# 640-point transform stages taken three slabs at a time instead of two

## The chip, the core and the metric

The kernel runs on one core of a Trainium2 chip. The metric is device time in microseconds (us), the median of three runs. A profiled execution is one run of its own; its span is the time between its first and last instruction.

## The reference

```
xn = layernorm(x)                                  # x: 2048 x 640, bf16
s  = irfft2(rfft2(xn) * (w_r + 1j*w_i))            # over rows and columns
g  = silu((gelu(xn @ w_gate) * (xn @ w_up)) @ w_down)   # 640 -> 1536 -> 640
out = x + s * g
```

So a spectral filter and a gated feed-forward network (FFN) run on the same normalized input and are multiplied at the end.

## The kernel before

The 2048 rows are held as 16 slabs of 128 rows. Both branches are matmuls. The FFN runs over four groups of four slabs: gate and up products (line 670: `psg`, `psu`), gelu on ScalarE into `ge` (L674), the product `uT` on VectorE (L676), and the down products (L694), whose result goes through tanh or silu into `G` (L702/L703, L699).

The Fourier branch has four stages, which are put in between the FFN's matmuls:

- Forward, per slab: `fold_a` and `fold_b` on VectorE add and subtract mirrored columns of `X` into a tile `f` (L443 to L453); `slab_S1` multiplies `f` with a table (`pz`, L481, five matmuls) and ScalarE copies it out as `Z` (L483). Per two slabs, `pair_D` calls `d_pair`: 128-row matmuls (L490) and then 32-row matmuls (L494) into `pd`, two PSUM tiles of two banks each. The two tiles are copied to `zd` with the columns spread by two (L502), and each slab is stored to DRAM scratch `ZDR` (L504).
- Frequency: `load_B2` reads `ZDR` back in ten DMAs (`B`, L522), in rows that hold all slabs; `pair_S2` multiplies (`px`, L532), copies (`xs`) and filters by `W1`, `W2` (L539); `pair_S2i` multiplies back (`pu`, L552) and stores to `UDR`.
- Inverse: `load_V` reads `UDR`; `slab_S1i` (`pv`, L597; `vs`, L599) per slab; `pair_Di` (again L490/L494) per two slabs, copied out as `eo` (L611); VectorE forms `cs` (L620) and `Yall` (L628/L629); `finish` multiplies by `G`, adds `x` and stores (L645 to L647).

Below, a call of `pair_D` or `pair_Di` is called a *turn*: within it TensorE goes over to 32-row matmuls and back.

The order is written by hand. A list `back` holds the FFN's pieces in order: 144 steps, numbered 0 to 143, each some five 512-column matmuls or eight 320-column ones. `put(s, f, ...)` hangs other work behind step `s`; that work is issued after the step's own matmuls, in the order of the `put` calls. Every engine takes its instructions in that order. The pool `psB` has two PSUM tiles, and `pz`, `pd`, `px`, `pu`, `pv` and the transposes all take turns in them; a turn takes both. Gate and up have two banks each. `load_B2` stands at step 54, the first `pair_S2` at 64, the second at 65, the inverse stage from step 96 (`vs0`). The tables are made in one scratch tile, `GEN`, whose parts are `vt` and `fv`; it, `B2` and `Vin` share one buffer after each other. All DMAs are issued by the SP queue, in order.

The step list of the forward stage, with `F0 = 30`:

```
for pair in range(8):
    a = F0 + 3 * pair
    put(a, slab_S1, 2 * pair)
    put(a + 1, slab_S1, 2 * pair + 1)
    put(a + 2, pair_D, pair)
```

Of the kernel before, what the change touches and what calls it, by code (L numbers as in the profile page):

```python
# [10 lines left out]
BF16 = mybir.dt.bfloat16  # L11
INT32 = mybir.dt.int32
ACT = mybir.ActivationFunctionType
ALU = mybir.AluOpType
P = 128
S = 2048
D = 640
L = 321
LP = 322
LH = 161  # L20
HD = 160
F = 1536
NT = F // P
NS = 16
# [7 lines left out]
def kernel(  # L32
# [40 lines left out]
    with tc.manual_schedule():  # L73
        build(nc, locals())


def build(nc, env):
    consts, big, wts, xg, work, psA, psB = (env[k] for k in ("consts", "big", "wts", "xg", "work", "psA", "psB"))
    ZDR, UDR, X, Wg, Wu, Wd, W1, W2 = (env[k] for k in ("ZDR", "UDR", "X", "Wg", "Wu", "Wd", "W1", "W2"))
# [52 lines left out]
    FT = consts.tile([P, 5, LH], BF16)  # L132
    FI = consts.tile([P, 5, LH], BF16)
# [8 lines left out]
    def gtile(shape, dt):  # L142
        n = 1
        for k in shape:
            n *= k
        w = n if dt != BF16 else n // 2
        ap = GEN[:, goff[0]:goff[0] + w]
        goff[0] += w
        assert goff[0] <= NH * L // 2
        if dt != INT32:  # L150
            ap = ap.bitcast(dt)
        if len(shape) > 1:
            names = "abcdefg"[:len(shape)]
            ap = ap.rearrange("p (%s) -> p %s" % (" ".join(names), " ".join(names)), **dict(zip(names, shape)))
        return ap
# [4 lines left out]
    done = set()  # L160
# [5 lines left out]
    xf = {}  # L166
# [50 lines left out]
    vt = gtile([NS, P], INT32)  # L217
# [111 lines left out]
    fv = gtile([10, LH], FP32)  # L329
# [125 lines left out]
    def chunk(f, k, c):  # L455
        return f[:, k, c * P:(c + 1) * P]
# [16 lines left out]
            nc.scalar.copy(out=xnT[g][:, :, j * P:(j + 1) * P], in_=pt)  # L473

    Zt = {}

    def slab_S1(n1):
        f = xf[n1 // 2]
        pz = psB.tile([P, 5, P], FP32, tag="b")
        for c in range(5):  # L480
            nc.tensor.matmul(pz[:, c, :], lhsT=chunk(f, n1 % 2, c), rhs=Tfwd[:, n1, :], start=True, stop=True)  # L481
        Zt[n1] = work.tile([P, 5, P], BF16, tag="m1", bufs=2, name=f"Z{n1}")
        nc.scalar.copy(out=Zt[n1], in_=pz)  # L483

    def d_pair(lhs, T, w):
        ps = [psB.tile([P, 2, 512], FP32, tag="b", name=f"pd{b}") for b in range(2)]
        out = [[ps[g // 2][:, g % 2, a * w:(a + 1) * w] for g in range(4)] for a in range(2)]
        for a in range(2):
            for g in range(4):
                nc.tensor.matmul(out[a][g], lhsT=lhs[a][:, g, :], rhs=T[:, g, 0:w], start=(a == 0), stop=False)  # L490
        for a in range(2):
            for g in range(4):
                r = slice(32 * g, 32 * g + 32)
                nc.tensor.matmul(out[a][g], lhsT=lhs[a][r, 4, :], rhs=T[r, 4, 0:w], start=False, stop=(a == 1))  # L494
        return [t[:, :, 0:2 * w].rearrange("p k (a m) -> p a k m", a=2) for t in ps]

    def pair_D(pair):
        pd = d_pair([Zt.pop(2 * pair + a) for a in range(2)], FT, LH)
        zd = work.tile([P, 2, 2, LP], BF16, tag="m2", bufs=2)
        for b in range(2):  # L500
            ev = nc.vector.tensor_copy if pair == 1 and b == 1 else nc.scalar.copy
            ev(out=zd.rearrange("p a c (m b) -> p a c m b", b=2)[:, :, :, :, b], in_=pd[b])  # L502
        for a in range(2):
            nc.sync.dma_start(out=ZDR[:, 2 * pair + a].rearrange("c p l -> p c l"), in_=zd[:, a, :, 0:L])  # L504

    warm_bank = []

# [52 lines left out]
    st_c = {}  # L560
# [4 lines left out]
    def load_V():  # L565
# [5 lines left out]
        st_c["V"] = V  # L571
        st_c["Y"] = big.tile([P, NS, D], BF16, tag="sX", name="Yall")

# [18 lines left out]
    def slab_S1i(n1):  # L592
        V = st_c["V"]
        pv = psB.tile([P, 5, P], FP32, tag="b")
        for c in range(5):
            lhsT = V[:, n1, VO[c]:VO[c] + P] if c < 4 else st_c[("r", n1)]
            nc.tensor.matmul(pv[:, c, :], lhsT=lhsT, rhs=Tinv[:, n1, :], start=True, stop=True)  # L597
        vs = work.tile([P, 5, P], BF16, tag="m1", bufs=2)
        nc.scalar.copy(out=vs, in_=pv)  # L599
        st_c[n1] = vs  # L600

    BY_SILU = (0, 3)
    Gt = {}
    Gok = set()

    def pair_Di(pair):
        n0 = 2 * pair
        py = d_pair([st_c.pop(n0 + a) for a in range(2)], FI, HD)
        eo = work.tile([P, 2, 2, 2, HD], BF16, tag="m2", bufs=2)
        for b in range(2):  # L610
            nc.scalar.activation(out=eo[:, b], in_=py[b], func=ACT.Copy,  # L611
                                 scale=(2.0 if n0 // 4 in BY_SILU else 1.0) / (S * D))
        st_c[("e", pair)] = eo

    def pair_cs(pair):
        eo = st_c.pop(("e", pair))
        st_c[("c", pair)] = cs = work.tile([P, 2, 2, 2, HD], BF16, tag="xf", bufs=2, name="cs")
        flat = "p a k n -> p (a k n)"
        for q, op in ((0, ALU.add), (1, ALU.subtract)):
            nc.vector.tensor_tensor(out=cs[:, q].rearrange(flat), in0=eo[:, 0].rearrange(flat),  # L620
                                    in1=eo[:, 1].rearrange(flat), op=op)

    def pair_Y(pair):
        n0 = 2 * pair
        cs = st_c.pop(("c", pair))
        Y = st_c["Y"][:, n0:n0 + 2, :].rearrange("p a (h n) -> p a h n", h=2)
        C, Z = (cs[:, :, :, k, :].rearrange("p h a n -> p a h n") for k in range(2))
        nc.vector.tensor_tensor(out=Y[:, :, :, 0:HD], in0=C, in1=Z, op=ALU.add)  # L628
        nc.vector.tensor_tensor(out=Y[:, :, ::-1, 319:159:-1], in0=C, in1=Z, op=ALU.subtract)  # L629
        for a in range(2):  # L630
            done.add(("y", n0 + a))

    left = {(n1, k) for n1 in range(NS) for k in range(2)}

# [3 lines left out]
    def finish(n1):  # L638
# [4 lines left out]
        G = Gt[n1 // 4]  # L643
        Y = st_c["Y"][:, n1, sl]
        nc.vector.tensor_tensor(out=Y, in0=Y, in1=G[:, n1 % 4, sl], op=ALU.mult)  # L645
        nc.vector.tensor_tensor(out=Y, in0=Y, in1=xts[n1][:, sl], op=ALU.add)  # L646
        nc.sync.dma_start(out=outv[n1][:, sl], in_=Y)  # L647
# [103 lines left out]
    def put(s, *item):  # L751
        plan[s].append(item)
# [35 lines left out]
    put(27, norm, 8)  # L788
    put(28, fold_b, 1)
    put(29, stats, 10)  # L790
    put(29, ft_sin, 1)
    put(29, mg_sin)
    put(29, mg_build)
    put(31, norm, 9)
# [12 lines left out]
    put(46, norm, 14)  # L807
    put(47, norm, 15)
    F0 = 30
    for pair in range(8):  # L810
        a = F0 + 3 * pair
        put(a, slab_S1, 2 * pair)
        put(a + 1, slab_S1, 2 * pair + 1)
        put(a + 2, pair_D, pair)
        if pair < 6:
            b = a if pair < 4 else a + 3
            put(b, fold_a, pair + 2)
            put(b + 1, fold_b, pair + 2)
    z_end = F0 + 24
    for k in range(4):  # L820
        put(32 + 3 * k, slab_T, 8 + k, 2)
# [15 lines left out]
    vs0 = sb + 8  # L837
    for i, at in enumerate((vs0 - 1, vs0, vs0 + 6, vs0 + 16, vs0 + 25)):
        put(at, gather, i)
    put(vs0 - 2, load_xt, 0)  # L840
    for pair in range(8):
        a = vs0 + 11 * pair // 2
        for k in range(2):
            put(a + 2 * k, slab_S1i, 2 * pair + k)
        if pair < 7:
            put(a + 4, load_xt, pair + 1)
        put(a + 4, pair_Di, pair)
        put(a + 5, pair_cs, pair)
        put(a + 6 if pair < 7 else a + 5, pair_Y, pair)
        for k in range(2):  # L850
            put(a + 7 + k if pair < 7 else a + 6, finish, 2 * pair + k)

    warm_pe(19)
    norm_parts(0)
# [43 lines left out]
```

## Time and profile before

| | us |
|---|---|
| three runs | 207.09, 207.86, 207.91 (median 207.86) |
| profiled execution | 207.12, span 205.3 |
| TensorE (PE) busy | 198.7 |
| VectorE (DVE) busy | 129.9 |
| ScalarE (ACT) busy | 124.7 |
| L502, copy of `pd` to `zd`, 128x644, 15 on ScalarE | 12.3, 883 ns each |
| L611, copy of `pd` to `eo`, 128x640, 16 | 10.4, 701 ns each |
| L483, copy of `pz` to `Z`, 128x640, 16 | 11.0, 694 ns each |
| L620, `cs`, 128x640, 16 | 7.1, 485 ns each |

In the profile's lines a group reads: line, engine, operation, tile written <- tiles read, shape, count, then busy time and the mean of one. A timeline line begins with start and length, and `[0.33 <-PE psg]` is idle time of the engine before it and what ended it. Lengths of matmuls overlap: the next one starts before the last has drained, so start to start is what counts. A few matmul records are missing from the trace, so a count may read x4 for five.

### The profile page before, as it was taken

What the parts mean: (1) busy time and instruction counts of PE and PEld (TensorE: products, weight loads), DVE (VectorE), ACT (ScalarE), POOL (GpSimd) and SP (SyncE); (2) the same over time, 40 slices, a digit from 0 to 9 for tenths busy, and PEclk for the clock granted to TensorE, in tenths of its full rate; (3) what the DMA queues carried; (4) which work ended last, traced back from release to release, by engine and by line L of the source; (5) the groups of instructions that cost most, each with busy time, mean ns of one, the idle gap of its engine ahead of it and who ended that gap; (6) DMA issues with size and microseconds to landing.
All of it is one profiled execution on the core that took longest, in us unless ns stands there. A gap on an engine that the chain in (4) does not pass through costs nothing.

```text
span 205.3 us, 4412 instructions
## 1 busy us (share of the span) xinstructions
PE 198.7 (97%) x1626; PEld 121.2 (59%) x1643; DVE 129.9 (63%) x357; ACT 124.7 (61%) x230; POOL 33.9 (17%) x61
## 2 busy tenths in 40 slices
PE   7999999999999999999999999999999999999993
PEld 5788855777555555475644444447775555556762
DVE  7886966797678842336565655433568768775653
ACT  2547567767868787225787777424555654656641
POOL 5328688945001100000000000000000000000000
PEclk9999999999999999999999999999999999999998
DMA  5999999899987799289965332369731332242111
GB/s 168 303 305 314 369 291 135 168 146 179 176 161 169 166 186 172 68 198 229 192 137 108 73 67 65 82 139 294 228 86 74 96 123 74 63 132 78 66 51 65
DMA packets 46199, 31.81 MB, mean 155 GB/s; under 512 B 12512, under 2 KB 43872, under 8 KB 46176
## 3 DMA queue, kind: packets, MB, share of 16 engines
q1 hardware_dynamic: 46176, 31.52, 67.1%
q8 instruction: 13, 0.21, 0.5%
q14 instruction: 10, 0.08, 0.1%
HBM read 21.66 MB, written 7.88 MB: 144 GB/s over the span
## 4 chain that ended last, share of the span: by engine, by line
PE 90%; DVE 4%; DMA 2%; issue 1%; ACT 1%; POOL 1%; SPq 0%; DVEq 0%
PE psu L670 24%; PE psg L670 24%; PE psg L694 13%; PE psu L694 12%; PE pd L490 5%; PE pu L552 3%; PE pv L597 2%; PE pz L481 2%; DMA X<-in_A_x_dram 2%; PE pd L494 2%; PE px L532 2%; DVE st L174 1%; DVE uT L676 1%; POOL rst L190 1%; PE pt L326 0%
## 5 line engine op out<-in xcount | busy, mean ns | idle before, releaser
L670 PE MATMUL psu<-xnT,Wu 128*128 128x512 bf16 (+2 forms) x289 | 60.4, 339 | 0.6 <-issue 0.3
L670 PE MATMUL psg<-xnT,Wg 128*128 128x512 bf16 (+2 forms) x284 | 59.9, 338 | 0.8 <-issue 0.3
L676 DVE TENSOR_TENSOR uT<-psu,ge 128x512 bf16<-128x512 f32 (+2 forms) x59 | 34.4, 586 | 33.7 <-PE psu L670 27.4
L674 ACT ACTIVATE ge<-psg 128x512 bf16<-128x512 f32 (+2 forms) x59 | 30.6, 518 | 28.9 <-PE psg L670 27.6
L694 PEld LDWEIGHTS <-uT 128*128 128x128 bf16 x384 | 36.1, 98 | 15.2 <-issue 0.5
L670 PEld LDWEIGHTS <-Wu 128*128 128x128 bf16 x295 | 26.5, 98 | 21.8 <-issue 1.3
L670 PEld LDWEIGHTS <-Wg 128*128 128x128 bf16 x295 | 26.2, 98 | 20.9 <-issue 1.0
L694 PE MATMUL psg<-Wd,uT 128*128 128x320 bf16 (+1 forms) x192 | 30.4, 303 | 0.0
L694 PE MATMUL psu<-Wd,uT 128*128 128x320 bf16 (+1 forms) x192 | 29.6, 296 | 0.0
L539 DVE TENSOR_TENSOR p<-xs,W 128x642 bf16<-128x642 bf16 x32 | 14.4, 492 | 8.9 <-ACT xs L535 8.5
L502 ACT CAST zd<-pd 128x644 bf16<-128x644 f32 x15 | 12.3, 883 | 4.6 <-PE pd L494 4.6
L611 ACT ACTIVATE eo<-pd 128x640 bf16<-128x640 f32 x16 | 10.4, 701 | 7.4 <-PE pd L494 7.4
L599 ACT CAST vs<-pv 128x640 bf16<-128x640 f32 x16 | 11.0, 690 | 6.1 <-PE pv L597 6.1
L174 DVE BATCH_NORM_STATS2 st<-X 128x6 f32<-128x320 bf16 x32 | 14.1, 481 | 0.3 <-issue 0.2
L535 ACT CAST xs<-px 128x642 bf16<-128x642 f32 x16 | 11.1, 692 | 4.0 <-PE px L532 3.6
L620 DVE TENSOR_TENSOR cs<-eo 128x640 bf16<-128x640 bf16 x16 | 7.1, 485 | 7.5 <-ACT eo L611 7.5
L483 ACT CAST Z<-pz 128x640 bf16<-128x640 f32 x16 | 11.0, 694 | 1.1 <-PE pz L481 1.1
L190 POOL TENSOR_TENSOR rst<-ve,mhalf 128x1 f32<-128x1 f32 (+2 forms) x9 | 6.5, 719 | 27.2 <-DVE ve L188 27.2
L645 DVE TENSOR_TENSOR Yall<-Yall,G 128x640 bf16<-128x640 bf16 (+3 forms) x18 | 8.1, 450 | 1.8 <-ACT G L699 1.6
L703 DVE SCALAR_TENSOR_TENSOR G<-th,psg 128x320 bf16<-128x320 f32 x8 | 3.9, 486 | 7.6 <-ACT th L702 7.6
L646 DVE TENSOR_TENSOR Yall<-Yall,xt 128x640 bf16<-128x640 bf16 (+3 forms) x18 | 8.2, 454 | 0.6
L552 PE MATMUL pu<-p,N 64*64 64x321 bf16 x128 | 8.2, 304 | 0.1
(138 smaller groups left out, 213.1 us busy)
## 6 DMA issues: line engine op xcount, KB each, us to landing
ZDR<-zd SPq DMA_DIRECT2D x16, 160.5 KB, 4.2
UDR<-us SPq DMA_DIRECT2D x32, 80.2 KB, 2.6
xt<-in_A_x_dram SPq DMA_DIRECT2D x8, 320.0 KB, 3.2
W<-in_A_w_r_dram SPq DMA_DIRECT2D x14, 160.5 KB, 6.8
W<-in_A_w_i_dram SPq DMA_DIRECT2D x14, 160.5 KB, 5.1
out_dram<-Yall SPq DMA_DIRECT2D x14, 160.0 KB, 1.8
B<-ZDR SPq DMA_DIRECT2D x6, 321.0 KB, 8.4
Vin<-UDR SPq DMA_DIRECT2D x6, 321.0 KB, 5.8
```

The costliest lines, as they stand in the source:

```text
L174: nc.vector.bn_stats(out=st[:, k, :], in_=X[:, n1, 320 * k:320 * k + 320])
L483: nc.scalar.copy(out=Zt[n1], in_=pz)
L502: ev(out=zd.rearrange("p a c (m b) -> p a c m b", b=2)[:, :, :, :, b], in_=pd[b])
L535: nc.scalar.copy(out=xs.rearrange("p (k l) -> p k l", k=2), in_=px[:, :, 0:L])
L539: nc.vector.tensor_tensor(out=pp, in0=xs, in1=WT[:, h].rearrange("p k l -> p (k l)"), op=ALU.mult)
L552: nc.tensor.matmul(pu[64 * lo:64 * lo + 64, hh, 0:L], lhsT=NM[r, kind, 0:64], rhs=pp[r, lo * L:(lo + 1) * L], start=first, stop=not first)
L599: nc.scalar.copy(out=vs, in_=pv)
L611: nc.scalar.activation(out=eo[:, b], in_=py[b], func=ACT.Copy, scale=(2.0 if n0 // 4 in BY_SILU else 1.0) / (S * D))
L670: nc.tensor.matmul(ps, lhsT=WT[:, c, t * P:(t + 1) * P], rhs=xnT[g][:, c, c0:c1_], start=(c == 0), stop=(c == 4))
L674: nc.scalar.activation(out=ges[t], in_=ps, func=ACT.Gelu_apprx_tanh)
L676: nc.vector.tensor_tensor(out=uT[g][:, t, c0:c1_], in0=ps, in1=ges[t], op=ALU.mult)
L694: nc.tensor.matmul(ph, lhsT=uT[g][:, t, j * P:(j + 1) * P], rhs=Wd[:, t, c0:c1_], start=(t == 0), stop=(t == NT - 1))
```

## The change

A turn now takes up to three slabs. Three slabs of 161 columns fill 483 of the 512 columns of a bank. Forward, the turns are slab 0 alone and then (1,2,3), (4,5,6) and so on to (13,14,15), at steps 29, 33, 38, 43, 48 and 53. Inverse, they are (0,1,2) to (12,13,14) and then slab 15 alone, at steps 102, 110, 118, 126, 134 and 138. `Z` and `zd` move to the table scratch (`fv`, `vt`), `vs`, `eo` and `cs` to the tile of the first filter, `W1`. `Z` and `vs` have four buffers. The second table sine, `ft_sin(1)`, moves from step 29 to 26. VectorE copies one half of the third turn, where before it copied one half of the second. The folds stay at their steps. The sums `cs` and `Yall` are put at steps of their own.

```diff
+    zbuf = fv.rearrange("p g l -> p (g l)").bitcast(BF16)[:, 0:4 * D].rearrange("p (s c k) -> p s c k", s=4, c=5)
+    zdbuf = vt.rearrange("p n k -> p (n k)").bitcast(BF16)[:, 0:12 * LP].rearrange(
+        "p (s a c l) -> p s a c l", s=2, a=3, c=2)
...
-        Zt[n1] = work.tile([P, 5, P], BF16, tag="m1", bufs=2, name=f"Z{n1}")
+        Zt[n1] = zbuf[:, n1 % 4]
...
-    def d_pair(lhs, T, w):
+    def d_group(lhs, T, w):
         ps = [psB.tile([P, 2, 512], FP32, tag="b", name=f"pd{b}") for b in range(2)]
+        n = len(lhs)
+        out = [[ps[g // 2][:, g % 2, a * w:(a + 1) * w] for g in range(4)] for a in range(n)]
+        for a in range(n):
             for g in range(4):
                 nc.tensor.matmul(out[a][g], lhsT=lhs[a][:, g, :], rhs=T[:, g, 0:w], start=(a == 0), stop=False)
+        for a in range(n):
             for g in range(4):
                 r = slice(32 * g, 32 * g + 32)
+                nc.tensor.matmul(out[a][g], lhsT=lhs[a][r, 4, :], rhs=T[r, 4, 0:w], start=False, stop=(a == n - 1))
...
+    DF = [(0, 1)] + [(n0, 3) for n0 in range(1, NS, 3)]
+    DG = [(n0, min(3, NS - n0)) for n0 in range(0, NS, 3)]
+
+    def group_D(i):
+        n0, n = DF[i]
+        pd = d_group([Zt.pop(n0 + a) for a in range(n)], FT, LH)
+        zd = zdbuf[:, i % 2, 0:n]
         for b in range(2):
+            ev = nc.vector.tensor_copy if i == 2 and b == 1 else nc.scalar.copy
             ev(out=zd.rearrange("p a c (m b) -> p a c m b", b=2)[:, :, :, :, b], in_=pd[b])
+        for a in range(n):
+            nc.sync.dma_start(out=ZDR[:, n0 + a].rearrange("c p l -> p c l"), in_=zd[:, a, :, 0:L])
...
-    put(29, ft_sin, 1)
+    put(26, ft_sin, 1)
...
+    for i, (n0, n) in enumerate(DF):
+        a = F0 - 2 if i == 0 else F0 + 5 * (i - 1)
+        for k in range(n):
+            put(a + k, slab_S1, n0 + k)
+        put(a + n, group_D, i)
+    for pair in range(6):
+        b = F0 + 3 * pair + (0 if pair < 4 else 3)
+        put(b, fold_a, pair + 2)
+        put(b + 1, fold_b, pair + 2)
...
+    put(vs0 + 4, load_xt, 1)
+    for i, (n0, n) in enumerate(DG):
+        a = vs0 + 8 * i
+        for k in range(n):
+            put(a + 2 * k, slab_S1i, n0 + k)
+        d = a + 6 if n == 3 else a + 2
+        put(d, group_Di, i)
+        for q in range(2):
+            put(d + 1 + (q if n == 3 else 0), group_cs, i, q)
+        for q in range(2):
+            put(d + (3 + q if n == 3 else 1), group_Y, i, q)
...
```

## The prediction

> **What bounds the kernel now.** I read the page first: busy times, slices, then the chain that ended last.
>
> ```profile
> PE 198.7 (97%) x1626; PEld 121.2 (59%) x1643; DVE 129.9 (63%) x357; ACT 124.7 (61%) x230; POOL 33.9 (17%) x61
> PEclk9999999999999999999999999999999999999998
> PE 90%; DVE 4%; DMA 2%; issue 1%; ACT 1%; POOL 1%; SPq 0%; DVEq 0%
> ```
>
> TensorE is the bound: 97% busy at full clock, 90% of the chain. Its queue is in order and nothing in it is spare, so whatever TensorE saves or waits moves the end by as much. ScalarE and VectorE, near 60%, count only where they make TensorE wait. So I priced the turn itself on the timeline of TensorE (start, length, instruction):
>
> ```profile
> 46.06 0.74 PE L490 MATMUL pd<-FT,Z 128*128 128x161 bf16 x8
> 46.73 0.32 PE L494 MATMUL pd<-FT,Z 32*128 32x161 bf16 x8
> 46.98 1.26 PE L694 MATMUL psg<-Wd,uT 128*128 128x320 bf16 x8
> ```
>
> A pair turn lasts 46.98 - 46.06 = 0.92 us. Then I looked for the places where the turn's neighbours are nearly late now: the first turn after ScalarE's table load, the fold that feeds slab 12, and the second frequency step.
>
> ```profile
> 52.73 1.28 ACT L674 ACT_TABLE_LOAD   x1
> 54.52 1.28 ACT L483 CAST Z<-pz 128x640 bf16<-128x640 f32 x2
> 55.54 0.91 PE L490 MATMUL pd<-FT,Z 128*128 128x161 bf16 x8
> ```
> ```profile
> 65.36 0.60 ACT L674 ACTIVATE ge<-psg 128x512 bf16<-128x512 f32 x1 [0.33 <-PE psg L670]
> 66.19 1.62 ACT L502 CAST zd<-pd 128x644 bf16<-128x644 f32 x2 [0.23 <-PE pd L494]
> 67.44 0.69 DVE L676 TENSOR_TENSOR uT<-psu,ge 128x512 bf16<-128x512 f32 x1 [0.93 <-PE psu L670]
> 70.36 0.22 DVE L453 TENSOR_TENSOR f<-uvt 128x128 bf16<-128x128 bf16 x1
> 71.90 0.44 PE L481 MATMUL pz<-Tfwd,f 128*128 128x128 bf16 x5
> ```
> ```profile
> 80.27 1.25 PE L670 MATMUL psg<-xnT,Wg 128*128 128x512 bf16 x5
> 80.37 1.62 ACT L502 CAST zd<-pd 128x644 bf16<-128x644 f32 x2 [1.00 <-PE pd L494]
> B<-ZDR SPq DMA_DIRECT2D x1, 240.8 KB, 5.8
> 93.96 0.33 PE L532 MATMUL px<-B,MG 64*64 64x321 bf16 x4
> ```
>
> See in the first group that the turn took 0.91 instead of 0.74: it waited for the second Z eviction, which ended at 55.80. In the second, slab 12's fold ended at 70.57 and TensorE came for it at 71.90: 1.33 to spare. In the third (the DMA row is the fourth load of B, issued at 87.91, so landed at 93.70), TensorE came for its rows at 93.96: 0.25 to spare.
>
> **The change, part by part.** Instructions set side by side: TensorE runs the same ones in both kernels, in another order; a bank holds three slabs, but each slab keeps its own matmuls. Nothing is saved in columns.
>
> *Fewer turns.* A slab costs four 128-row matmuls of 0.071 each (eight are 0.57 in the chain) and one round of four 32-row ones; in the records a second slab's round starts 0.07 after the first's, and is 0.01 wide. That is 0.368 a slab, 0.736 a pair, so 0.92 - 0.736 = 0.184 a turn is fixed: the switch to 32-row form and back. Sixteen turns become twelve: 4 x 0.184 = 0.74 saved, on the path. Predicted triple turn: 3 x 0.368 + 0.184 = 1.29.
>
> *First turn after the table load (now slabs 4 to 6, step 38).* Step 28 ends at 41.15 now; after it come slab 0's transform 0.28, step 29 with 1.09, the single turn 0.55, steps 30 to 33 with 4.35, three transforms 0.84 and a triple 1.29: 49.55. The five steps and three transforms to the next turn end at 55.81. ScalarE then evicts its two banks of 966 elements. No row shows 966; the 644 form is 0.883, and with some 0.18 fixed (plain evictions of 320 and 640: 0.437 and 0.690) it scales to 1.235; if the extra for the spread-out write were fixed, 1.14. I take 1.235, a pair overlapped 2.35 (now 1.62), ending at 52.03. Two silu G (0.33 apart), Z4, table load 1.28, ge, Z5 and Z6 follow and end near 56.25; the third matmul of the turn, whose bank that frees, would come at 55.96. Wait 0.29, against 0.17 now: +0.12 (0 to 0.25).
>
> *Slab 12's fold.* The fold keeps its step 46, but slab 12's first transform moves from 48 to 47, and the D turn before it (step 47) goes. On VectorE the fold comes 3.13 after the start of the uT product of step 45 (67.44 to 70.57): product, mean, fold_a, norm behind a POOL power, fold_b. Measure from the end E of the turn that moves to step 43. The uT product needs ge of step 44, and on ScalarE that now stands behind the two evictions: E+0.10, +2.35, ge 0.60 (0.10 overlapped) gives E+2.95, uT at E+3.0, fold done at E+6.13. TensorE comes for slab 12 after four halves of 1.079 and two transforms of 0.279, at E+4.87, and can end its last chunk 0.15 after the fold, at E+6.28 instead of E+5.15. Wait: 1.1. If ge were not late, uT would start at E+2.43 and the wait be 0.6; if evictions and ge queue slightly more, 1.3.
>
> The Trainium skill (TensorEngine Tiling (Array Packing), section PSUM Bottleneck) warns of this kind of cost: after row tiling the copy out of PSUM may become the bottleneck. This trace has ScalarE at 61%, so over the span it does not; by that rule only the place of the queue, not its load, is the trouble.
>
> *The way through DRAM.* The last turn stays at step 53, but with three slabs. From its end, 80.27 now: evictions done 1.74 later; two stores, issued 0.40 apart, landing 3.0 and 3.4 after issue; the first B load at 85.93, the fourth landing at 13.43, TensorE asking at 13.69. After the change: evictions done after 2.45 (+0.71, or +0.51 by the cheaper price). Then three stores; no row shows a third. Issues are 0.4 to 0.5 apart, and the two landings 0.82 apart (85.04, 85.86): the third lands 0.4 to 0.8 later. I take 0.5, nearer the issue spacing, as the queue is freer: the last eight loads of W2 then go out before the turn of step 48. Together +1.2, less 0.25 of cover: wait 0.95 (0.4 to 1.5). The steps of the frequency stage did not move, so nothing else absorbs it.
>
> The Trainium skill (DMA: Bandwidth & Descriptors, Anatomy of one DMA — SWDGE (gpsimd) path) fits a DMA on that path as 2.0 us plus its bytes over 436,000 a microsecond. Its 0.38 for 160.5 KB, an estimate by that page, set in for the third store would make the wait 0.83; the two landings here are 0.82 apart, about twice that.
>
> *Free edits.* The rest has cover. Slab 0 and the early ft_sin: POOL had the sine's input ready at 33.25, and Tfwd and the fold of slab 0 were there at 39.42 and 37.7, before step 28 ends at 41.15. Four Z buffers and the W1 scratch: W1's last reader is the last filter product, long over; the scratch in GEN is freed by the same stores that B waits for anyway. Inverse stage: evictions of 960, some 0.95 each, fall into two steps (2.2) before the next transform, so the banks are free; VectorE's sums go from 32 at 0.485 to 20 near 0.65 and 4 at 0.33, 1.2 less, off the path. At the end slab 15 alone follows its turn; its sums take 1.0 and slabs 13 and 14 (0.97 each) end by 201, before G of slab 15 at 201.4. If one of these covers failed it would cost about one eviction, 0.7 to 1.2.
>
> *Sum.* -0.74 + 0.12 + 1.1 + 0.95 = +1.43. The profiled execution took 207.12, the runs 207.09, 207.86 and 207.91, so the profiled one is 0.74 under the median; the mean of the four is 207.5. I put the sum on that: 208.9. (On the profiled execution's own basis it is 208.55, on the median 209.3.) About 0.5%, 1.04 us, is what can be told from no change.
>
> **Rivals.**
> 1. *The stores are not late (not slower).* If the third landing follows the second by so little that the fourth B load is at most 0.25 later, TensorE never waits there: -0.74 + 0.12 + 1.1 = +0.48, 208.0, no change. The deciding point for "not slower" is a wait under 0.56, so a delay under 0.8. For it: the freer queue. Against it: the evictions alone bring 0.5 to 0.7. Chance 0.18.
> 2. *The fold is in time.* If ge were not behind the evictions in effect and VectorE ran ahead, -0.74 + 0.12 + 0.95 = +0.33, 207.8. Against it: the order on both engines is fixed, and VectorE was idle 0.93 before that uT, so it is bound to it. Chance 0.1.
> 3. *Neither wait comes* and only turns count: -0.74, or -0.9 with the table-load wait gone too: 206.6 to 206.8. It would pass 0.5% if a turn's fixed price were 0.26 rather than 0.184. For it: both waits come from times worked out to some 0.3 us. Against it: both have little cover now. Chance 0.1, half of it over 0.5% faster.
> 4. *More queues collide*: 966-element evictions hold both banks, and every turn waits some 0.2 for its last Z: 12 x 0.2 = 2.4 on top of 1.43 makes 211.3. Against it: of the eight turns before, only the one after the table load waits for its last Z. Chance 0.07.
> The whole change does take place: the built program has twelve turns.
>
> **The numbers.** My forecast has 0.55: sum +0.3 to +2.2 over bases 207.1 to 207.9, likeliest 208.9; three parts in four of it, 0.41, lie over +1.04. With rival 4 (0.07) and a fifth of rivals 1 and 2, whose bases may be high (0.06), slower gets 0.54; faster 0.05 from rival 3; the rest is 0.41. The range 207.0 to 210.4 takes in rivals 1 and 2 and leaves out rival 4 and most of rival 3.
>
> **What would show it.** Turns: twelve, triples at 1.29. A gap on TensorE of about 1.1 ahead of slab 12's transform, with ge of step 44 behind two evictions of about 1.24. A gap of about 0.95 ahead of the second px, ended by a landing of B. A wait of 0.3 in the turn after the table load. No new gap in the inverse stage. A gap in the inverse stage, or a turn over 1.4, would make the forecast wrong from that side; no gap at px or slab 12 from the other.

## The result, and the profile after

The changed kernel takes 208.25 us (median of 22 runs, 207.67 to 209.18), the kernel before 207.22 beside it (22 runs): a ratio of 1.0046, 95% interval 1.0033 to 1.0058, so 0.95 us slower (0.7 to 1.2). The forecast was 208.9 and +1.43. The sign is the forecast's; at 0.46% the size lies just under the bound of 0.5%, where the prediction had 0.54 over it and 0.41 within. The profiled execution took 208.22 (span 206.3), against 207.12 (span 205.3).

The page's busy line, clock row and chain by engine:

```profile
PE 198.2 (96%) x1627; PEld 121.5 (59%) x1643; DVE 128.9 (62%) x349; ACT 123.6 (60%) x224; POOL 33.9 (16%) x61
PEclk9999999999999999999999999999999999999998
PE 76%; DMA 9%; DVE 6%; issue 3%; ACT 2%; SPq 2%; POOL 1%; DVEq 0%
```

TensorE is still the bound and has the same work at the same clock, but the chain leaves it more often. The timeline of TensorE (start, length, instruction) shows the new turn:

```profile
48.46 1.02 PE L494 MATMUL pd<-FT,GEN 128*128 128x161 bf16 x12
49.42 0.39 PE L498 MATMUL pd<-FT,GEN 32*128 32x161 bf16 x12
49.74 0.72 PE L712 MATMUL psg<-Wd,uT 128*128 128x320 bf16 x4
```

49.74 - 48.46 = 1.28 us for three slabs (forecast 1.29); the single turn took 0.57. Next, the steps from 36 to the turn after the table load at step 38:

```profile
51.93 0.44 PE L484 MATMUL pz<-Tfwd,f 128*128 128x128 bf16 x5
52.60 1.25 PE L688 MATMUL psg<-xnT,Wg 128*128 128x512 bf16 x4 [0.24 <-DMA xnT<-X]
56.41 1.02 PE L494 MATMUL pd<-FT,GEN 128*128 128x161 bf16 x12
57.69 1.04 PE L688 MATMUL psu<-xnT,Wu 128*128 128x512 bf16 x3
```

The turn itself (56.41 to 57.69) waits for nothing, but step 36 starts at 52.60 where slab 4's transform, 0.28 long, left room at 52.21: it waited 0.40 for the transposed loads of slabs 4 to 7. This wait was not in the forecast. Then slab 12's fold, first ScalarE and VectorE, then TensorE:

```profile
65.32 2.35 ACT L510 CAST GEN<-pd 128x966 bf16<-128x966 f32 x2 [1.36 <-PE pd L498]
67.51 0.61 ACT L692 ACTIVATE ge<-psg 128x512 bf16<-128x512 f32 x1
68.15 0.69 DVE L694 TENSOR_TENSOR uT<-psu,ge 128x512 bf16<-128x512 f32 x1 [0.92 <-ACT ge L692]
71.07 0.22 DVE L453 TENSOR_TENSOR f<-uvt 128x128 bf16<-128x128 bf16 x1
```
```profile
69.02 1.24 PE L688 MATMUL psu<-xnT,Wu 128*128 128x512 bf16 x5
70.74 0.23 PE L484 MATMUL pz<-Tfwd,f 128*128 128x128 bf16 x1 [0.47 <-DVE f L452]
71.21 0.40 PE L484 MATMUL pz<-Tfwd,f 128*128 128x128 bf16 x4 [0.24 <-DVE f L452]
71.44 1.24 PE L688 MATMUL psg<-xnT,Wg 128*128 128x512 bf16 x5
```

The Gelu stands behind two wide copies (2.35, as forecast), uT behind the Gelu, the fold behind uT. From 69.02, a half (1.08) and a transform (0.28) would end at 70.38; the next step starts at 71.44: 1.06 lost (forecast 1.1). Last, the way through DRAM (the DMA row is the fourth load of B, issued at 90.98):

```profile
81.43 2.34 ACT L510 CAST GEN<-pd 128x966 bf16<-128x966 f32 x2 [1.36 <-PE pd L498]
```
```profile
B<-ZDR SPq DMA_DIRECT2D x1, 240.8 KB, 4.5
```
```profile
95.02 0.33 PE L540 MATMUL px<-B,MG 64*64 64x321 bf16 x2
95.50 0.33 PE L540 MATMUL px<-B,MG 64*64 64x321 bf16 x2 [0.16 <-DMA B<-ZDR]
95.51 0.59 PE L560 MATMUL pu<-p,N 64*64 64x321 bf16 x8
96.03 1.26 PE L712 MATMUL psg<-Wd,uT 128*128 128x320 bf16 x8
```

The second px waits 0.48 for that load (forecast 0.95). It costs less: from the first px row to the next step is 1.01 here and 0.87 without a wait, because the second half of pu's matmuls waits for a product of VectorE (p2, the second `p`) anyway.

### The profile page after: what moved, and what is told of

Read it like the earlier page. It is cut to its first block, busy times and chain, and to the rows that moved or that the text cites. A ratio compares the mean times of both kernels' runs of the same rounds, so it can differ in the third digit from the quotient of the medians.

```text
span 206.3 us, 4389 instructions
## 1 busy us (share of the span) xinstructions
PE 198.2 (96%) x1627; PEld 121.5 (59%) x1643; DVE 128.9 (62%) x349; ACT 123.6 (60%) x224; POOL 33.9 (16%) x61
## 4 chain that ended last, share of the span: by engine, by line
PE 76%; DMA 9%; DVE 6%; issue 3%; ACT 2%; SPq 2%; POOL 1%; DVEq 0%
PE psu L688 22%; PE psg L688 21%; PE psg L712 9%; PE psu L712 9%; PE pd L494 4%; PE pu L560 3%; DMA xnT<-X 2%; DMA B<-ZDR 2%; PE pv L605 2%; DMA X<-in_A_x_dram 2%; DMA ZDR<-GEN 2%; PE px L540 2%; PE pz L484 2%; PE pd L498 2%; ACT GEN L510 1%
## 5 line engine op out<-in xcount | busy, mean ns | idle before, releaser
L688 PEld LDWEIGHTS <-Wg 128*128 128x128 bf16 x295 | 26.8, 99 | 22.6 <-issue 1.0
L510 ACT CAST GEN<-pd 128x966 bf16<-128x966 f32 (+1 forms) x11 | 11.5, 1112 | 5.4 <-PE pd L498 5.4
L607 ACT CAST W<-pv 128x640 bf16<-128x640 f32 x16 | 11.0, 689 | 4.7 <-PE pv L605 4.7
L486 ACT CAST GEN<-pz 128x640 bf16<-128x640 f32 x16 | 11.0, 696 | 3.9 <-PE pz L484 3.9
L630 ACT ACTIVATE W<-pd 128x960 bf16<-128x960 f32 (+2 forms) x14 | 10.1, 780 | 5.2 <-PE pd L498 5.2
L636 DVE TENSOR_TENSOR W<-W 128x960 bf16<-128x960 bf16 (+1 forms) x12 | 6.8, 598 | 3.1 <-ACT W L630 3.0
L484 PEld LDWEIGHTS <-f 128*128 128x128 bf16 x80 | 5.8, 98 | 4.1 <-DVE f L452 1.3
```

The lines of the kernel that those rows point to most:

```text
L630: nc.scalar.activation(out=eo[:, b, :, a0:a1].rearrange("p k a n -> p a k n"), in_=py[b][:, a0:a1], func=ACT.Copy, scale=(2.0 if silu[a0] ...
L688: nc.tensor.matmul(ps, lhsT=WT[:, c, t * P:(t + 1) * P], rhs=xnT[g][:, c, c0:c1_], start=(c == 0), stop=(c == 4))
```

## The experiments

Each kernel was timed in five rounds beside the kernel before, except e12_before, which ran once, for its trace.

### Slab 12's fold: e1_fold_early, e5_late_bank, e6_norm_later

```diff
-        b = F0 + 3 * pair + (0 if pair < 4 else 3)
+        b = F0 + 3 * pair + (0, 0, 0, 0, 2, 3)[pair]
```

> The changed kernel with one edit: the fold of slabs 12 and 13 (fold_a, fold_b of pair 6) is issued one step earlier, at steps 44 and 45 instead of 45 and 46. Theory: the 1.06 us for which TensorE waited at step 47 for f is a position on VectorE's queue and goes away; step 54 then begins 1.06 earlier, and the forward filter's stores keep their distance to the last turn, so that the wait before px stays near 0.5 us. The time is then 1.06 below the changed kernel: about 207.2, the kernel before's time. Rival: the stores and the W2 loads on SP's queue do not move with the PE stream, so the wait before px grows by what the fold gives back, and the time falls by 0.5 us or less (207.7 or more).

Measured 206.76 against 207.13, ratio 0.9985 (0.9971 to 0.9999): 1.1 to 1.3 us under the two measurements of the changed kernel (1.0046 and, below, 1.0039). TensorE at the same place:

```profile
68.86 1.24 PE L688 MATMUL psu<-xnT,Wu 128*128 128x512 bf16 x5
69.94 0.44 PE L484 MATMUL pz<-Tfwd,f 128*128 128x128 bf16 x5
70.22 1.24 PE L688 MATMUL psg<-xnT,Wg 128*128 128x512 bf16 x5
```

From psu to the next psg 1.36 us, against 2.42 in the changed kernel: all 1.06 came back, and the px wait did not grow (there was none). The rival falls. What made the wait is split by the next two.

```diff
+        evict(0)
+        if i == 3:
+            later.extend((lambda: evict(1), store))
+            return
...
+        if i == 3:
+            put(a + n + 1, late_bank)
```

(later holds the copy and the stores, and late_bank runs them.)

> The changed kernel with one edit: of the third three-slab turn (slabs 7 to 9) the second bank's copy and the three stores are issued one step later, behind the Gelu of step 44, so that ScalarE's 2.35 us pair of copies no longer stands ahead of that Gelu. It tells how much of the 1.06 us fold wait is the wide copy and how much the earlier place of slab_S1(12). Theory: uT's multiply then waits for psu, which ends 0.5 us sooner than the Gelu did, and the fold is ready 0.5 sooner, as in the kernel before; the rest of the wait, 0.5 to 0.6, is slab_S1(12) having moved ahead of its fold and stays. Time 0.5 below the changed kernel: 207.7. Rival: the wide copy is all of it (VectorE idled 0.92 for that Gelu); the wait falls below 0.2 and the time by 0.9: 207.3.

```diff
-    put(46, norm, 14)
+    put(47, norm, 14)
```

> The changed kernel with one edit: the normalisation of slab 14, which stands on VectorE between fold_a and fold_b of slabs 12 and 13 and waits 0.19 us for GpSimd's power there, is issued one step later (47 instead of 46). Theory: fold_b starts 0.19 + 0.45 sooner, the wait at step 47 falls from 1.06 to about 0.45, and the time by 0.6: 207.6. Rival: TensorE is held there by something that is not VectorE's order (the copy of pz, the banks), the wait stays and the time with it: 208.2.

```profile
69.11 1.24 PE L703 MATMUL psu<-xnT,Wu 128*128 128x512 bf16 x5
70.33 0.23 PE L484 MATMUL pz<-Tfwd,f 128*128 128x128 bf16 x1
70.80 0.40 PE L484 MATMUL pz<-Tfwd,f 128*128 128x128 bf16 x4 [0.24 <-DVE f L452]
71.03 1.24 PE L703 MATMUL psg<-xnT,Wg 128*128 128x512 bf16 x5
```

That is e5_late_bank: 71.03 - 69.11 = 1.92, a wait of 0.56 as its theory had it. Its rival, that the wide copy is all of the wait, falls. In e6_norm_later the same two rows stand at 70.37 and 72.29, again 1.92 and 0.56, where 0.45 was expected. The ratios are 1.0035 (1.0023 to 1.0047; 207.72) and 1.0025 (1.0011 to 1.0039; 207.51), below the changed kernel's by less than the half microsecond of the traces; the intervals are as wide as that difference. So the Gelu's place behind the wide copies is half of the wait. The other half is there with the Gelu in time, as slab_S1(12) comes a step earlier than before; the norm between the folds is half a microsecond of the same chain.

### The two halves of the change: e3_inverse_only, e4_forward_only

e3_inverse_only is the kernel before with only the inverse half of the change (first line), e4_forward_only with only the forward half (second line):

```diff
+        py = d_group([st_c.pop(n0 + a) for a in range(n)], FI, HD)
...
+        pd = d_group([Zt.pop(n0 + a) for a in range(n)], FT, LH)
```

> The kernel before with the second half of the change alone: the inverse stage in five turns of three slabs and one of one, with its buffers in the first filter; the forward stage in pairs as before. Theory: the inverse turns save 0.42 us of TensorE and the order of the last finishes gives 0.14 back at the end: 0.28 below the kernel before, about 206.9. Rival: the saving is lost at the end, where VectorE closes the work: no change, 207.2.

> The kernel before with the first half of the change alone: the forward stage in one turn of one slab and five of three, with its buffers in the table scratch; the inverse stage in pairs as before. Theory: the forward stage costs what it showed in the trace, +1.06 at step 47, +0.14 net at px, -0.38 from the turns, and +0.2 at the table load and the transposed loads before it: about 1.2 above the kernel before, 208.4, and slower than the whole change by what the inverse stage saves. Rival: the 0.40 us wait for the transposed loads of slabs 4 to 7 was a matter of that one execution, and then it is 0.8 above, 208.0.

Measured 206.99, ratio 0.9991 (0.9981 to 1.0002), and 208.43, ratio 1.0054 (1.0037 to 1.0072). By these ratios the inverse half gains about 0.2 and the forward half costs about 1.1; together +0.93, the whole change's 0.95, so nothing shows that the halves act on each other. e3's 0.2 and e4's 1.1 agree with both theories within their intervals, but neither rival (no change; 0.8) is excluded by the time. For e3_inverse_only the trace helps: from the end of the last forward turn to the modelled end of TensorE's last matmul are 121.12 us, against 121.55 and 121.56 in the two traces of the kernel before. The turns do save 0.43 there, as its theory has it.

### The way through DRAM: e2_last_split, e11_again, e12_before

```diff
-            ev = nc.vector.tensor_copy if i == 2 and b == 1 else nc.scalar.copy
+            ev = nc.vector.tensor_copy if i in (2, 5) and b == 1 else nc.scalar.copy
```

> The changed kernel with one edit: in the last forward turn (group_D, i = 5) the second bank is copied by VectorE instead of ScalarE, so that both 966-point copies run at once and the last stores are issued about 1.1 us earlier. Theory: the second B load lands about 1.1 earlier and TensorE's 0.48 us wait before the second px goes; but pair_S2i's second half there waits on p2 in the kernel before too, so the end moves by 0.15 to 0.3 us only: about 208.0. Rival 1: the wait was a plain 0.48 on the path and all of it comes back, 207.75. Rival 2: the loads are held by the transfers ahead of them and not by the stores' issue, the wait stays, and the time does not move: 208.2.

Measured 208.23, ratio 1.0054 (1.0037 to 1.0072): no gain at all. In the trace there is no px wait, the fourth load landing 0.69 ahead of TensorE. But it is not shown that the edit took the wait away: the first of the last three stores is issued 1.0 us sooner (2.74 after the start of the last turn, 3.75 in e11_again below), yet the fourth load lands only 0.24 sooner (14.28 and 14.52), and e4_forward_only, without this edit, has 0.74 of cover. So the reason of rival 2, that something other than the stores' issue holds the loads, may well be right; what it is was not tried. That raised the question whether the wait is there at all in most executions. Both kernels went again, unaltered:

> The changed kernel once more, unaltered, beside the kernel before on this chip and with a second profiled execution. Theory: the fold wait of 1.06 us at step 47 is there again, since two orders of instructions make it; the 0.48 us wait before the second px, which none of the other traces with three-slab forward turns shows, is not; the wait for xnT at step 36 is between 0 and 1.6. Time 1.0 above the kernel before. Rival: the px wait is the changed kernel's own and shows again at 0.4 to 0.6.

> The kernel before once more, unaltered, for a second profiled execution. In its first trace the fourth load of B landed 13.43 us after the last forward turn, 0.25 us before TensorE came for it; in e3_inverse_only, whose forward stage is the same, 11.35 after it, 2.36 before. Theory: the 0.25 of cover from which the px term was worked out belonged to that one execution, and the usual cover with pair turns is nearer 2 us; it shows 1.5 or more here. TensorE's third fetch of instructions comes at 43 to 45 us and step 36 does not wait for xnT. Rival: 0.25 is usual, and e3_inverse_only was the exception; it shows under 0.8.

e11_again: 208.08, ratio 1.0039 (1.0022 to 1.0057), TensorE's rows:

```profile
52.41 1.25 PE L688 MATMUL psg<-xnT,Wg 128*128 128x512 bf16 x5 [0.23 <-DMA xnT<-X]
70.54 0.23 PE L484 MATMUL pz<-Tfwd,f 128*128 128x128 bf16 x1 [0.47 <-DVE f L452]
71.01 0.40 PE L484 MATMUL pz<-Tfwd,f 128*128 128x128 bf16 x4 [0.24 <-DVE f L452]
94.82 0.33 PE L540 MATMUL px<-B,MG 64*64 64x321 bf16 x4
95.02 0.73 PE L560 MATMUL pu<-p,N 64*64 64x321 bf16 x8
```

The fold wait is there again (psu at 68.82, the next psg at 71.25: 2.43, so 1.07); px runs without a gap. Then e12_before, the fourth load of B (issued at 87.43) and the second px:

```profile
B<-ZDR SPq DMA_DIRECT2D x1, 240.8 KB, 4.3
```
```profile
93.84 0.33 PE L532 MATMUL px<-B,MG 64*64 64x321 bf16 x4
```

The load took 4.3 us, not the 5.8 of the trace that the prediction read, and landed at 91.72: 2.1 us of cover, where that trace had 0.25. With e3_inverse_only's 2.4, two of three pair-turn traces have over 2. In the eleven traces with three-slab forward turns the cover is 0.06 to 0.74 in nine, and two wait (the changed kernel's first, and e9_pad below by 0.4). So the change does use up some 1.5 to 2 us of cover there (against the two pair-turn traces that have it), and mostly that is all it does.

### The transposed loads: e8_xn_first, e9_pad

e8_xn_first moves the last first-filter loads behind them, on top of e1_fold_early; e9_pad is the changed kernel with more instructions ahead on TensorE's queue:

```diff
-        put(8 + k if k < 8 else (32, 35, 38, 41, 44, 44, 47, 47)[k - 8], w_rows, k // 8, k % 8 // 4, k % 2, k % 4 // 2)
+        put(8 + k if k < 6 else 24 if k < 8 else (32, 35, 38, 41, 44, 44, 47, 47)[k - 8], w_rows, k // 8, k % 8 // 4, k % 2, k % 4 // 2)
```
```diff
-    warm_pe(19)
+    warm_pe(15)
+    warm_pe(16, 64)
```

> The fold one step early as in e1_fold_early, and the last four loads of the first filter (w_rows k = 6 and 7, some 2 us of transfers) issued at step 24, behind the transposed loads of slabs 4 to 7, instead of ahead of them. Theory: the transposed loads land 1 to 2 us sooner, the 0.37 us wait for them at step 36 goes, and nothing else is late for the filter rows: 206.4. Rival: the transposed loads start no sooner, since their sources or the queue's own slots hold them, and the time stays: 206.76.

> The changed kernel with one edit at the start: of TensorE's 19 warming matmuls four are replaced by sixteen short ones of 64 columns, which take as long but put 24 more instructions ahead of everything else on TensorE's queue. In the traces so far TensorE's third fetch of instructions (one 16 KB transfer of queue q8, at 45.9 us or later with three-slab forward turns, at 44.3 and 44.7 with pairs) is followed, wherever it falls on the transposed loads of slabs 4 to 7, by 1.2 to 1.5 us in which hardly a byte is moved, and step 36 then waits for xnT. Theory: the place of the fetch follows from TensorE's instructions; it comes some 1.5 us earlier, among the first filter's loads, the pause and the wait go, and the turn of step 38 waits 0.24 for Z6 instead: 0.2 to 0.4 below the changed kernel, 207.9 to 208.1. Rival: the fetch comes when the transfers ahead of it let it, wherever TensorE is; it stays at 46 to 49 and the time at 208.2.

In neither trace does step 36 wait for xnT, and neither kernel gained: 206.89, ratio 0.9991 (0.9982 to 1.0000), no better than e1_fold_early, and 208.05, ratio 1.0037 (1.0020 to 1.0055), beside 208.08 of e11_again. For e8_xn_first the edit accounts for it: the four transposed loads land at 43.81 to 46.87, in e1_fold_early at 49.61 to 52.40. For e9_pad that is not shown: e2_last_split and e7_tail, which change nothing there, do not wait in their traces either (last landings 51.89 and 51.80; 51.09 in e9_pad, 52.56 in the changed kernel). TensorE in e9_pad shows where the time went:

```profile
56.48 0.88 PE L494 MATMUL pd<-FT,GEN 128*128 128x161 bf16 x10 [0.24 <-ACT GEN L486]
```

With step 36 on time, the turn of step 38 waits for its last Z, as the prediction had it. From step 36 to the end of that turn is 5.48 us (52.13 to 57.61) instead of 5.08 in e11_again (52.41 to 57.49), so the wait is 0.40; and 0.40 is what step 36 had lost in the changed kernel. One wait stands in for the other: up to 0.40, late transposed loads cost nothing. (e4_forward_only lost 1.1 there, so 0.7 net, and e6_norm_later 1.7, so 1.3 net, in their profiled executions.)

### The end: e7_tail, e10_both

```diff
-            put(min(d + (5 + k if n == 3 else 2), vs0 + 44), finish, n0 + k)
+            put(d + 4 if n0 + k in (12, 13) else min(d + (5 + k if n == 3 else 2), vs0 + 44), finish, n0 + k)
```

> The fold one step early as in e1_fold_early, and the finishes of slabs 12 and 13 issued at step 138, ahead of the half finish of slab 14 that waits for its G. Theory: VectorE's 2.0 us of idle time before that wait is filled, the last 448-column multiply starts when its G is there, 0.1 to 0.2 sooner, and the end moves by as much: 206.6, against 206.76 of e1_fold_early. Rival: the end is set by the last G and the store behind it alone; no change from e1_fold_early.

> The three edits that helped or cost nothing together: the fold one step early (e1_fold_early), the finishes of slabs 12 and 13 ahead of slab 14's half (e7_tail), and the last first-filter loads behind the transposed loads (e8_xn_first). Theory: no wait at step 47 and none at step 36, the turns' 0.8 us kept but for 0.07 at step 38 and 0.1 at the end: 0.5 below the kernel before in the profile, 206.6. Rival: e8_xn_first gained nothing in the time because the execution's end is held elsewhere; then it is 206.8, as e7_tail.

VectorE near the end, the changed kernel and then e7_tail:

```profile
198.26 0.32 DVE L663 TENSOR_TENSOR Yall<-Yall,G 128x320 bf16<-128x320 bf16 x1 [2.02 <-ACT G L717]
202.38 0.38 DVE L663 TENSOR_TENSOR Yall<-Yall,G 128x448 bf16<-128x448 bf16 x1
```
```profile
198.88 0.32 DVE L664 TENSOR_TENSOR Yall<-Yall,xt 128x320 bf16<-128x320 bf16 x1
200.81 0.39 DVE L663 TENSOR_TENSOR Yall<-Yall,G 128x448 bf16<-128x448 bf16 x1 [1.61 <-ACT G L717]
```

In the first, VectorE idles 2.02 us for slab 14's G with slabs 12 and 13 queued behind it, and then runs without a gap to the end; in the second it is done early and waits for the last G. From the modelled end of TensorE's last matmul to the last landing is 2.65 us in the changed kernel and 2.51 in e7_tail, as in the kernel before (2.51). The time, 206.83, ratio 0.9981 (0.9972 to 0.9990), does not resolve that 0.13 from e1_fold_early.

e10_both measured 206.52 against 207.11, ratio 0.9963 (0.9949 to 0.9978): faster than the kernel before by 0.59 between the medians (0.77 by the ratio), and than the changed kernel beside it by 1.56. The theory's 206.6 holds. At 0.37% the gain is small, but its interval is clear of no change; it overlaps e7_tail's, so what the earlier transposed loads add to the other two edits is not resolved. It is the version to keep.

## Why the prediction was right, and where not

Right in direction; the time, 0.65 below the forecast, lies well in the range, and two of its four terms met their rows.

- *Fewer turns.* Forecast -0.74. Forward 5 x 1.28 + 0.57 = 6.97 for 8 x 0.92 = 7.36, inverse 5 x 1.26 + 0.56 = 6.86 for 8 x 0.91 = 7.28: about -0.8. The fixed price per turn (0.184) held.
- *Slab 12's fold.* Forecast +1.1, measured 1.06 and 1.07, and e1_fold_early took it away. The prediction's split held too: it gave 0.6 without a late Gelu, and e5_late_bank showed 0.56.
- *First turn after the table load.* Forecast a wait of 0.29 against 0.17; measured 0.40 wherever nothing ahead of it was late, so +0.23. The first trace hid it behind the xnT wait, which no step of the prediction had.
- *The way through DRAM.* Forecast +0.95: this is the term that was mis-sized, and it is 0 in nine of eleven traces and 0.1 net in the two that wait. The delay was not overrated (forecast 1.2, found 1.5 to 2). What failed is "0.25 to spare": it came from one landing, and that execution's fourth load was 1.5 us slower than the others'. A second error made the price of a wait too high as well: pu's own wait for p2 behind px covers some 0.35 of it, and the prediction did not look there.
- *Free edits.* The end was held to be covered; it cost 0.13.
- *The base.* The sum was put on 207.5, the mean of four; 22 runs give 207.22. That is 0.28 of the 0.65.

Of the 208.9, then, the surviving sum is -0.8 + 0.23 + 1.06 + 0.13 = +0.62. The last landings in e11_again and e12_before, 204.90 and 204.22, stand 0.68 apart, 0.10 of it from the start. The runs' difference is 0.3 larger. Part lies outside the spans (time less span is 1.97 and 2.06 in the two traces of the changed kernel, 1.78 and 1.77 in those of the kernel before, and anything from 1.78 to 2.13 in the ten others), part in executions with a longer xnT wait or a px wait; how much is whose stays open.

Rival 1 (stores not late, +0.48, 208.0, given 0.18) came nearest in outcome: TensorE does not wait at px as a rule. Its reason did not hold: the landings are later by 1.5 to 2 us, and it was the cover that was larger. That the forecast's size came out as well as it did is in part luck: part of the 0.95 that was not there was made up by terms that it had too low or not at all (0.11 more at step 38, 0.13 at the end) and by the 0.3 that stays open. Rival 4 is out: no other turn waits for its last Z, and the inverse stage shows no gap.

The rule of the Trainium skill that was weighed (TensorEngine Tiling (Array Packing), PSUM Bottleneck) fits in the narrow sense only: ScalarE is 60% busy, as before, and what the wide copy cost, 0.5, was its place ahead of one Gelu. The 0.38 for the third store, the estimate by the Trainium skill's figures (DMA: Bandwidth & Descriptors, Anatomy of one DMA — SWDGE (gpsimd) path), comes from a fit of that path, and here SP issues the stores. It is short of ten of the eleven traces, where the third landed 0.52 to 1.59 after the second (0.53 in the first trace); in e10_both it was 0.17.

## What to carry to other kernels

A cover is a difference of two times, and where one of them is a DMA landing it belongs to one execution: before a term is built on it, look for the same landing in another row or run, and give the term a range down to nothing. When a step is moved, read its feeder's queue order on the other engines: the largest loss went when a fold was issued one step earlier, and the trace shows no new wait for it. And two waits in a row on the same queue need not add up: at steps 36 and 38 the later one was shortened by what the earlier one took.

## What was not expected of the hardware

TensorE's instructions arrive in 16 KB transfers on a DMA queue of their own (q8: thirteen in every trace or, with 1626 matmuls and 1643 weight loads, one for about 250 instructions). That they are TensorE's is borne out by e9_pad: with 24 more instructions ahead, the second of these fetches starts at 25.9, in the other thirteen traces at 26.9 to 27.2. Where the third falls on the transposed loads, the data stand still. The DMA view of the changed kernel from 47.5 to 48.5 us (queue q8), and its packets from 48.25 to 49.5; then e9_pad's packets from 48.25 to 49.5:

```profile
q8 instruction: 1, 0.02, 6.7%
```
```profile
DMA packets 40, 0.01 MB, mean 8 GB/s; under 512 B 40, under 2 KB 40, under 8 KB 40
```
```profile
DMA packets 1272, 0.31 MB, mean 248 GB/s; under 512 B 1272, under 2 KB 1272, under 8 KB 1272
```

The fetch ran from 47.63 to 48.69, and for 1.25 us after 48.25 the sixteen engines moved 8 GB/s in place of 248. The pause is there, for 1.0 to 1.4 us, in all eight traces in which the third fetch is under way while the transposed loads run fast, the engines together at 190 GB/s or more (early and harmless in e8_xn_first and e10_both), and in none of the six in which it had ended before that, by 0.7 us or more. So the two come together; that the fetch makes the pause is argued from this and not shown.

Nor is the place of the third fetch set by TensorE's instruction count alone. e9_pad's came at 43.39, without a pause: earlier, as its theory asks, but by 4.0 us against 47.40 in e11_again, where some 1.5 were expected. But in the eight traces that have the changed kernel's forward instructions and loads unaltered up to there it comes anywhere from 45.87 (e7_tail, without a pause) to 48.96 (e6_norm_later). And e8_xn_first and e10_both, which add no instruction and only put four filter loads behind the transposed ones, have it at 44.26 and 45.31. So the transfers ahead of it bear on it as well, as the rival to e9_pad says. Why the transposed loads stop, and plain loads in flight with a fetch (43.4 in e9_pad) do not, is open.

The Trainium skill (Runtime: NRT & Kernel Launch, Instruction fetch mechanics) has the block of 16 KiB or 256 instructions and a DMA queue of the sequencer's own, and calls the cost mostly hidden. The size agrees. No idle time of TensorE here is put down to a fetch, as the page has it; of the data queue's pause of 1.25 us it says nothing.
